# Top-k attention with a mixture of depths: slot search on GpSimd, the last products and the scatter one step sooner, and plain writes of the last rows

## The chip, the core and the metric

The kernel runs on one core of a Trainium2 chip. The core has a matrix engine (TensorE, PE in the profile, with its weight loads shown apart as PEld), a vector engine (VectorE, DVE), an activation engine (ScalarE, ACT), a general engine (GpSimd, POOL) and a queue for transfers (SyncE, SP). Each engine executes its own list of instructions in order and waits on semaphores for the others. The metric is the device time of one execution in microseconds; lower is better.

## The reference

There are 8 batches of 8 heads, 576 tokens and 64 features a head. Attention keeps, in each row, the 32 largest scores:

```python
scores = scale * np.matmul(q, k.transpose(0, 1, 3, 2))
kth = np.partition(scores, -top_k, axis=-1)[..., -top_k:-top_k + 1]
scores = np.where(scores >= kth, scores, -1e9)
attn = exp(scores - max) / sum            # then out = attn @ v
```

The heads' outputs of a batch, side by side, are `x` of 576 x 512. The second part, the mixture of depths, takes the 128 tokens of the batch with the largest gate score and adds to them a gated two-layer product:

```python
scores = x @ w_gate                        # one number a token
top_idx = 128 largest tokens of the batch
ye = np.maximum(x[top_idx] @ w1, 0.0) @ w2 # 512 -> 1024 -> 512
g = 1.0 / (1.0 + np.exp(-scores[top_idx]))
out[top_idx] = x[top_idx] + g[:, None] * ye
```

All other rows of `out` are `x`.

## The kernel before

**Units and steps.** A unit is a pair of heads with 128 rows of scores (or four half tiles for the last 64 rows). A batch has 18 units, the whole problem N = 144. The main loop goes over steps `n` from -1 to 143, and what follows writes i for `n % 18`. In step n every engine works on a different unit: TensorE multiplies the scores of unit n+1 (`multiply`), ScalarE copies them from PSUM to the tile `sc` (`keep`), VectorE searches unit n for a bound on the 32nd largest score (`find_bound`: 16 MAX8 on 72 columns each into `cand`, then MAX8 and MATCH_REPLACE8 on the candidates into `best`), ScalarE and GpSimd turn unit n-1 into `y`, the scores below that bound (`what_is_below`: `sides` is a sign with its count, `y` the product of scores and signs, `fill` 16 more columns), VectorE finds the exact 32nd largest of unit n-2 by two MAX8 on `y` (`find_kth`, result `next`), ScalarE and GpSimd each make half of the mask `less` of unit n-3 (`mask`), and TensorE transposes unit n-4 with the mask, ScalarE takes the exponential (`pT`, `last`) and TensorE multiplies it with the values into `av`.

**The order is written out by hand.** Engines are wrapped in `InOrder`, so the order of the code is the order on each engine. Three lists hold work to be put between: `vector_late` is flushed between the two halves of `find_bound`'s first loop (and after it), `late` goes to ScalarE ahead of `keep`, and `pool_late` goes to GpSimd after `find_bound` and ahead of `what_is_below`.

**Loads.** The rows of k and q of the next batch are transposed in half loads, one or two in a step, into the free columns of the score bank, and copied out by ScalarE (`kT`, `qT`). `loads_at[i]` says how many in step i, `first_loads` the same for the first batch; a batch has 18 of them.

**The mixture.** `mixture` is a generator of one batch, advanced at the end of those steps that `mix_at` lists (`mix_at_of` for the last two that run in the main loop), counted from the start of the following batch. Its stages are: `split` of the gates, and a row of all gates on every partition (`gate_row`); for each of 5 tiles of tokens `choose`, which counts how many gates are greater (`junk`, the rank in `ranks`) and then compares the rank with 0 to 127 (`pick`, the slot of each token); `multiply_places`, which turns picks into row numbers on TensorE; `fetch_rows`, a gather into `xe`; the transposes `xeT`; eight steps of `multiply_h`; eight of the product `y_ps`; then the scaled result `gy` on ScalarE and `add_rows`, an indirect DMA from GpSimd that adds 128 rows to `out` in memory. In a step with that scatter GpSimd is spared its half of the mask, which VectorE takes instead: the line `scatters = n % per_batch == 1 and n > 2 * per_batch`, so n = 37, 55, 73, 91, 109 and 127. `gates` is a dot product on VectorE (`prod` in the profile) for each tile of tokens that is done, after `normalise` (a reciprocal `rden`, then `x` on GpSimd).

**The tail.** After the loop the last four units are finished in an order of their own, and `closing` runs the mixture of the last batch, where each stage waits for the one before. Remaining stages of the batch before it, named `between`, are put in the gaps.

Of the kernel before, what the change touches and what calls it, by code (L numbers as in the profile page):

```python
# [10 lines left out]
AF = mybir.ActivationFunctionType  # L11
ALU = mybir.AluOpType
# [34 lines left out]
def kernel(  # L47
# [13 lines left out]
    B, H, S, D = q.shape  # L61
    HD = H * D
    F = moe_w1.shape[1]
    NHP = H // 2
# [7 lines left out]
    scale = 1.0 / float(D) ** 0.5 / SMALLER  # L72
# [92 lines left out]
    def load_weights():  # L165
# [6 lines left out]
    pe, dve, act, pool, sp = (  # L172
        InOrder(tc, e)
        for e in (nc.tensor, nc.vector, nc.scalar, nc.gpsimd, nc.sync)
    )


    late, vector_late, pool_late = [], [], []
# [410 lines left out]
    def mixture(row0, pg, rank, exact=False):  # L589
# [8 lines left out]
        if exact:  # L598
            for t0, t1, at in ((0, J, 0), (J, NT, JP)):
                tr = ps_misc.tile([P, 512], FP32, name="tr", tag="misc")  # L600
                n = R if t0 else P
# [6 lines left out]
                w = (t1 - t0) * n  # L608
                act.copy(out=gate_row[:, at : at + w], in_=tr[:, 0:w])
        else:  # L610
            row_dram = drampool.tile([1, S], FP32, name="row_dram")
            sp.dma_start(
                out=row_dram[0, 0:JP].rearrange("(p j) -> p j", j=J), in_=gate[:, 0:J]
            )
            sp.dma_start(
                out=row_dram[0, JP:S].rearrange("(p j) -> p j", j=1),
                in_=gate[0:R, J:NT],
# [5 lines left out]
        for t in range(NT):  # L623
            yield
            n = R if t == J else P

            def choose(t=t, n=n):
                junk = modpool.tile([P, S], FP32, name="junk", tag="scratch")
                dve.tensor_scalar(
                    out=junk[0:n, :],  # L630
                    in0=gate_row[0:n, :],
                    scalar1=gate[0:n, t : t + 1],
                    scalar2=None,
                    op0=ALU.is_gt,
                    op1=ALU.add,
                    accum_out=rank[0:n, t : t + 1],
                )
                if exact:
                    break_ties(t, gate, gate_row, rank)
                dve.tensor_scalar(  # L640
                    out=pick[0:n, t, :],
                    in0=slot[0:n, :],
                    scalar1=rank[0:n, t : t + 1],
                    scalar2=None,
                    op0=ALU.is_equal,
                )

            vector_late.append(choose)

        yield  # L650
        if exact:
            ps = ps_misc.tile([P, 512], FP32, name="place_ps", tag="misc")
        else:
            ps = values_bank[0]
        ps = ps[:, 2 * DE : 2 * DE + 6]
# [3 lines left out]
        row_i = modpool.tile([P, 1], I32, name="row_i", bufs=2)  # L659
        g = modpool.tile([P, 1], FP32, name="g", bufs=2)  # L660
# [27 lines left out]
        xe = modpool.tile([P, HD], FP32, name="xe")  # L688
# [4 lines left out]
        ps = ps_misc.tile([P, 512], FP32, name="xe_ps", tag="misc")  # L693
# [8 lines left out]
        for fc in range(NFC):  # L702
# [3 lines left out]
            if fc % 2 == 0:  # L706
                ps = ps_misc.tile([P, 2, CAP], FP32, name="h_ps", tag="misc")
# [8 lines left out]
        for fc in range(NFC):  # L716
            yield
            if fc == 0:
                ps = ps_misc.tile([P, 512], FP32, name="y_ps", tag="misc")
# [3 lines left out]
        gy = modpool.tile([P, HD], FP32, name="gy")  # L723
# [5 lines left out]
    def closing(b, pg, between):  # L729
# [51 lines left out]
        for t in range(J):  # L781
            dve.tensor_scalar(
                out=pick[:, t, :],
                in0=slot,
                scalar1=rank[:, t : t + 1],
                scalar2=others[:, t : t + 1],
                op0=ALU.subtract,
# [53 lines left out]
        for fc in range(NFC):  # L841
            pe.matmul(
                ps, hT[:, fc, :], w2[:, fc, :], start=(fc == 0), stop=(fc == NFC - 1)
            )
        gy = modpool.tile([P, HD], FP32, name="gy")
        w = HD // 2
        act.activation(gy[:, 0:w], ps[:, 0:w], AF.Copy, scale=g)
        dve.tensor_scalar_mul(gy[:, w:HD], ps[:, w:HD], g[:, 0:1])
        add_rows(gy, row_i)

    def multiply_places(ps, pick, pg):

# [45 lines left out]

    def add_rows(gy, row_i):

        pool.indirect_dma_start(
            out=out.flatten_outer_dims(),
            out_offset=bass.IndirectOffsetOnAxis(ap=row_i, axis=0),
            in_=gy,
            in_offset=None,
            compute_op=ALU.add,
        )

    def multiply_h(ps, fc, xeT):
# [38 lines left out]
    def store(ob, x):  # L948
# [11 lines left out]
    v_at = 6  # L960


    mix_at = (5, 7, 9, 10, 13, 14, 16, 16, *range(19, 34), 35, 36)


    mix_at_of = {
        B - 3: mix_at[0:8] + (19, 20, 20, 21, 21, 22, 22, 23, 24)
        + (25, 26, 26, 27, 27, 28, 28, 29),
        B - 2: (5, 7, 7, 8, 8, 8, 10, 10, 12, 13, 14, 15, 15, 16, 16, 17, 17),
    }  # L970

    loads_at = [1, 0, 0, *[1] * 11, 2, 2, 1, 1]
    first_loads = [0, 0, 1, *loads_at[3:]]
    assert sum(loads_at) == sum(first_loads) == 2 + 4 * NHP
    mix_steps = {}
    for b in range(B - 1):
        for i in mix_at_of.get(b, mix_at):
            mix_steps.setdefault((b + 1) * per_batch + i, []).append(b)

    place_steps = {}  # L980
    for b in range(B - 1):
# [51 lines left out]
    def mask_of(n, on=None):  # L1033
        b, i = divmod(n, per_batch)
        masks[n] = mask(scs[n], next8s[b][:, i, :, :], on)
        if i == per_batch - 1:
            at = 2 * per_batch * b
            pool.tensor_copy(
                out=seen[:, 1, at : at + 2 * per_batch].rearrange("p (n i) -> p n i", i=2),
                in_=next8s.pop(b)[:, :, :, 7],  # L1040
            )

    for n in range(-1, N):
        b, i = divmod(n, per_batch)
        if i == 0 and 0 <= b < B - 1:
            qkv[b + 1] = room_for_qkv(b + 1)
            loading = chain(
                loading, Rows(k[b + 1], q[b + 1], *qkv[b + 1][0:2]).parts()
            )
        if 0 < n + 1 < NHP:  # L1050
            turn_pair(first_rows, n + 1)
        if n == 1:
            load_v(v[0], qkv[0][2])
        if n == NHP:
            load_weights()


        gating = normalised
        if inverting is not None:
            normalised = inverting[0:2]  # L1060
            vector_late.insert(0, lambda a=inverting: normalise(*a))
            inverting = None
        else:
            normalised = None
        if gating is not None:
            vector_late.append(lambda a=gating: gates(*a))

        if is_unit(n - 4):  # L1070
            tr, av = room_to_turn()
            pT, last, exp = weigh(scs.pop(n - 4), tr, av, masks.pop(n - 4))
            exp()
        if is_unit(n - 3):

            scatters = n % per_batch == 1 and n > 2 * per_batch
            mask_of(n - 3, (act, dve) if scatters else None)
        flush()
        if is_unit(n + 1):
            b, t, g = units[n + 1]  # L1080
            ps = room_for_scores()
            multiply(t, g, *qkv[b][0:2], ps)
            b, i = divmod(n, per_batch)
            loads = list(islice(loading, first_loads[i] if b == 0 else loads_at[i]))
            halves = [ps[:, a, :, HALF : HALF + P] for a in range(2)]
            for load, half in zip(loads, halves):
                load[0](half)
            scs[n + 1] = keep(ps)
            for load, half in zip(loads, halves):
                load[1](half)  # L1090
        if is_unit(n - 4):
            b4, t4, g4 = units[n - 4]
            values(t4, g4, pT, last, av, qkv[b4][2])
            if n in place_steps:
                values_bank[0] = av
                next(mixtures[place_steps[n]])
            if g4 == 0:
                xs = xpool.tile([P, H, DE], FP32, name="xs")
                if t4 == 0:
                    x = xpool.tile([P, NT, HD], FP32, name="x")  # L1100
                    pg = gates_of[b4 % 2]
                    of_batch[b4] = x, pg
            keep_values(t4, g4, av, xs)
            if g4 == groups(t4) - 1:
                inverting = b4, t4, xs
                n4 = R if t4 == J else P
                keep_sums(n4, xs, sums[0:n4, b4 * NT + t4, :])
            while kept:
                kept.pop(0)()


        if is_unit(n):
            bests[n] = find_bound(scs[n])
        flush_vector()
        flush_pool()
        if is_unit(n - 2):
            kth_of(n - 2)
        while after_kth:
            after_kth.pop(0)()


        if is_unit(n - 1):
            what_is_below(n - 1)

        if gating is not None:
            b, t = gating
            if t == J:
                store(out[b], of_batch[b][0])
                mixtures[b] = mixture(float(b * S), of_batch[b][1], ranks[:, b, :])
        for b in mix_steps.get(n, ()):  # L1130
            next(mixtures[b], None)
        b, i = divmod(n, per_batch)
        if i == v_at and 0 <= b < B - 1:
            load_v(v[b + 1], qkv[b + 1][2])
# [55 lines left out]
    closed = closing(B - 1, pg, between)  # L1190
    next(closed)
    values_unit(N - 1)
    for _ in range(3):
        next(between)
    keep_unit(N - 1, xs)
    sums_of(J, xs)
# [156 lines left out]
```

## Time and profile before

| | before |
|---|---|
| time, median of 3 runs | 859.5 us (858.61 to 859.57) |
| span of the profile | 858.1 us |
| start of step 18, 36, 54, ... 126 on VectorE | 111.0, 210.4, 309.2, 408.0, 506.8, 605.6, 704.4 us |
| one batch in the steady part | 98.8 us |
| start of step 143, the last of the loop | 800.1 us |
| VectorE, ScalarE, GpSimd busy | 808.5, 761.0, 708.1 us |

In the profile's page, part 1 gives the busy time of each engine, part 5 the groups of equal instructions with their mean duration and the idle time ahead of them with what ended it. The stretches view gives the same busy times in windows of time, the waits view sums up who waited for whom, and the timeline lists instructions in order of start. On VectorE instructions overlap: the next starts before the last one's end is recorded. So what an instruction costs is the distance from its start to the start of the next, and not its duration.

### The profile page before, as it was taken

What the parts mean: (1) busy time and instruction counts of PE and PEld (TensorE: products, weight loads), DVE (VectorE), ACT (ScalarE), POOL (GpSimd) and SP (SyncE); (2) the same over time, 40 slices, a digit from 0 to 9 for tenths busy, and PEclk for the clock granted to TensorE, in tenths of its full rate; (3) what the DMA queues carried; (4) which work ended last, traced back from release to release, by engine and by line L of the source; (5) the groups of instructions that cost most, each with busy time, mean ns of one, the idle gap of its engine ahead of it and who ended that gap; (6) DMA issues with size and microseconds to landing.
All of it is one profiled execution on the core that took longest, in us unless ns stands there. A gap on an engine that the chain in (4) does not pass through costs nothing. (4 is left out here: it accounts for less than half of the span.)

```text
span 858.1 us, 28073 instructions
## 1 busy us (share of the span) xinstructions
PE 797.7 (93%) x9839; PEld 613.0 (71%) x9839; DVE 808.5 (94%) x4932; ACT 761.0 (89%) x1705; POOL 708.1 (83%) x699
## 2 busy tenths in 40 slices
PE   5799988988999999999999999999999999998976
PEld 4576666666787778877787777877788778767844
DVE  5899999999999999999999999999999999999850
ACT  3799999999999999999999999999999999978720
POOL 3599899888898899988898899988998888978720
PEclk9699999999999999999999999999999999999998
DMA  9921212421151221412233212512214102101021
GB/s 175 277 53 27 52 45 51 89 46 39 51 97 32 51 39 57 108 39 50 64 60 68 52 26 70 100 23 50 69 38 97 26 16 63 22 11 17 3 71 25
DMA packets 122196, 50.36 MB, mean 59 GB/s; under 512 B 116416, under 2 KB 116416, under 8 KB 121024
## 3 DMA queue, kind: packets, MB, share of 16 engines
q1 hardware_dynamic: 118672, 43.91, 21.9%
q0 software_dynamic: 1792, 4.20, 2.8%
q8 instruction: 79, 1.29, 0.6%
q14 instruction: 69, 0.57, 0.2%
q10 hardware_dynamic: 1584, 0.39, 0.2%
HBM read 36.93 MB, written 11.55 MB: 56 GB/s over the span
## 5 line engine op out<-in xcount | busy, mean ns | idle before, releaser
L43 POOL TENSOR_TENSOR y<-sc,sides 128x576 f32<-128x576 f32 x288 | 367.9, 1304 | 99.4 <-ACT sides L43 91.9
L43 DVE MAX8 cand<-sc 128x8 f32<-128x72 f32 x2304 | 330.2, 218 | 11.1 <-ACT sc L43 11.1
L43 POOL TENSOR_SCALAR less<-sc,next 128x576 bf16<-128x576 f32 x135 | 236.3, 1750 | 7.7 <-DVE next L43 5.0
L43 ACT ACTIVATE sides<-sc,seen 128x576 bf16<-128x576 f32 x288 | 221.0, 768 | 5.2
L43 PE MATMUL ptr<-out_of_reach,less 128*128 128x128 bf16 x1136 | 205.4, 220 | 19.6 <-POOL less L43 18.9
L43 PE MATMUL ptr<-ident,sc 128*128 128x128 f32 x1136 | 215.8, 280 | 0.0
L43 DVE MAX8 next<-y 128x8 f32<-128x584 f32 x288 | 204.5, 751 | 4.4 <-POOL y L43 4.3
L43 PE MATMUL ps<-kT,qT 64*128 64x288 f32 (+1 forms) x1280 | 184.6, 437 | 7.1 <-ACT qT L43 5.3
L43 PEld LDWEIGHTS av<-v,pT 128*64 128x64 f32 x4544 | 144.2, 137 | 46.1 <-ACT last L43 33.5
L43 PEld LDWEIGHTS ptr<-ident,sc 128*128 128x128 f32 x1136 | 160.8, 142 | 22.6 <-PE av L43 10.4
L43 PE MATMUL av<-v,pT 128*64 128x65 f32 x4544 | 163.9, 224 | 13.2 <-ACT last L43 11.8
L43 ACT COPY sc<-ps 128x1152 f32<-128x1152 f32 x144 | 160.6, 1115 | 11.8 <-PE ps L43 11.0
L43 PEld LDWEIGHTS <-less 128*128 128x128 bf16 x1296 | 133.3, 104 | 40.8 <-POOL less L43 26.0
L43 ACT ACTIVATE pT<-ptr 128x1024 f32<-128x1024 f32 x142 | 143.9, 1014 | 19.0 <-PE ptr L43 16.2
L43 DVE MAX8 best<-cand 128x8 f32<-128x24 f32 (+2 forms) x864 | 141.9, 200 | 0.0
L43 PEld LDWEIGHTS ps<-kT,qT 64*128 64x128 f32 (+1 forms) x1280 | 99.9, 180 | 46.8 <-issue 22.2
L43 ACT ACTIVATE less<-sc,next 128x576 bf16<-128x576 f32 x143 | 110.7, 774 | 12.6 <-DVE next L43 12.4
L43 DVE MATCH_REPLACE8 cand<-best,cand 128x24 f32<-128x24 f32 (+1 forms) x576 | 101.9, 185 | 0.0
L43 PE MATMUL av<-vpair,last 128*128 128x130 f32 (+1 forms) x314 | 68.1, 317 | 0.0
L43 PE MATMUL h_ps<-xeT,w 128*128 128x128 f32 x464 | 61.3, 277 | 0.3 <-ACT xeT L43 0.3
L43 PEld LDWEIGHTS h_ps<-xeT,w 128*128 128x128 f32 x464 | 55.8, 192 | 2.5 <-ACT xeT L43 1.4
L43 PE MATMUL y_ps<-w,hT 128*128 128x512 f32 x112 | 56.3, 596 | 0.0
(124 smaller groups left out, 848.2 us busy)
## 6 DMA issues: line engine op xcount, KB each, us to landing
v<-in_v_dram SPq DMA_DIRECT2D x64, 128.0 KB, 3.3
out_dram<-x SPq DMA_DIRECT2D x8, 1024.0 KB, 4.1
rows<-in_k_dram SPq DMA_DIRECT2D x56, 128.0 KB, 3.2
rows<-in_q_dram SPq DMA_DIRECT2D x56, 128.0 KB, 3.1
w<-in_moe_w_dram SPq DMA_DIRECT2D x2, 2048.0 KB, 13.5
gate_row<-row_dram SPq DMA_DIRECT2D x7, 288.0 KB, 4.5
w<-in_k_dram SPq DMA_DIRECT2D x8, 128.0 KB, 4.4
last<-in_k_dram SPq DMA_DIRECT2D x8, 128.0 KB, 3.6
```

Source lines behind the costliest of these rows:

```text
L43: return lambda *a, **kw: self._tc.keep_in_program_order(fn(*a, **kw))
```

## The change

There are four edits.

1. **Slots on GpSimd.** In `choose` the count stays on VectorE. The comparison that makes `pick` becomes `choose_slot`: tile 0 keeps it on VectorE, and the other four tiles of each batch put it into `pool_late`, so that GpSimd makes it after `find_bound` of the same step.
2. **One step sooner.** `mix_at` ends with steps 34 and 35 in place of 35 and 36, so the last two products, `gy` and the scatter come one step earlier (the scatter at i = 0, where it was at i = 1). `scatter_steps` now names the steps whose mask half VectorE takes: n = 54, 72, 90, 108, 126 and 137. Step 37, which had no scatter, is gone from it, and 137 is new. One half load moves from i = 16 to i = 1, with the stream of loads one behind.
3. **Last mixtures sooner.** `mix_at_of` begins most stages of the mixtures of batches 5 and 6 a step sooner. One stage of `between` moves from the gap before the last row's `keep_unit` to the loop in `closing` that finishes it.
4. **Last rows written.** In `closing` one VectorE instruction makes `gy = ps * g + xe`, in place of half a product on ScalarE and half on VectorE, and the rows are written over those in memory (`put_rows`) instead of being added there.

```diff
-                dve.tensor_scalar(
+                if t == 0:
+                    choose_slot(dve, t, n)
+                else:
+                    pool_late.append(lambda: choose_slot(pool, t, n))
+
+            def choose_slot(engine, t, n):
+                engine.tensor_scalar(
                     out=pick[0:n, t, :],
...
-        w = HD // 2
-        act.activation(gy[:, 0:w], ps[:, 0:w], AF.Copy, scale=g)
-        dve.tensor_scalar_mul(gy[:, w:HD], ps[:, w:HD], g[:, 0:1])
-        add_rows(gy, row_i)
+        dve.scalar_tensor_tensor(
+            out=gy, in0=ps, scalar=g[:, 0:1], in1=xe, op0=ALU.mult, op1=ALU.add
+        )
+        put_rows(gy, row_i)
...
-    mix_at = (5, 7, 9, 10, 13, 14, 16, 16, *range(19, 34), 35, 36)
+    mix_at = (5, 7, 9, 10, 13, 14, 16, 16, *range(19, 36))
...
-        B - 3: mix_at[0:8] + (19, 20, 20, 21, 21, 22, 22, 23, 24)
-        + (25, 26, 26, 27, 27, 28, 28, 29),
-        B - 2: (5, 7, 7, 8, 8, 8, 10, 10, 12, 13, 14, 15, 15, 16, 16, 17, 17),
+        B - 3: mix_at[0:8] + (18, 19, 20, 21, 21, 22, 23, 24, 24)
+        + (25, 25, 26, 26, 27, 27, 28, 28),
+        B - 2: (5, 6, 6, 7, 7, 7, 9, 9, 11, 12, 13, 14, 15, 16, 16, 17, 17),
...
-    loads_at = [1, 0, 0, *[1] * 11, 2, 2, 1, 1]
+    loads_at = [1, 1, 0, *[1] * 11, 2, 2, 0, 1]
...
+    scatter_steps = {
+        (b + 1) * per_batch + mix_at_of.get(b, mix_at)[-1] + 1 for b in range(B - 2)
+    }
...
-            scatters = n % per_batch == 1 and n > 2 * per_batch
-            mask_of(n - 3, (act, dve) if scatters else None)
+            mask_of(n - 3, (act, dve) if n in scatter_steps else None)
...
-    for _ in range(3):
+    for _ in range(2):
         next(between)
```

More of the change, by code (lines that the diff above doesn't have):

```diff
@@ L899, in add_rows, with put_rows @@
     def add_rows(gy, row_i):
+        put_rows(gy, row_i, compute_op=ALU.add)
+    def put_rows(rows, row_i, **how):
         pool.indirect_dma_start(
@@ L903, in add_rows @@
             out_offset=bass.IndirectOffsetOnAxis(ap=row_i, axis=0),
-            in_=gy,
+            in_=rows,
             in_offset=None,
-            compute_op=ALU.add,
+            **how,
         )
@@ L960 @@
     v_at = 6
-    mix_at = (5, 7, 9, 10, 13, 14, 16, 16, *range(19, 34), 35, 36)
+    mix_at = (5, 7, 9, 10, 13, 14, 16, 16, *range(19, 36))
     mix_at_of = {
-        B - 3: mix_at[0:8] + (19, 20, 20, 21, 21, 22, 22, 23, 24)
-        + (25, 26, 26, 27, 27, 28, 28, 29),
-        B - 2: (5, 7, 7, 8, 8, 8, 10, 10, 12, 13, 14, 15, 15, 16, 16, 17, 17),
+        B - 3: mix_at[0:8] + (18, 19, 20, 21, 21, 22, 23, 24, 24)
+        + (25, 25, 26, 26, 27, 27, 28, 28),
+        B - 2: (5, 6, 6, 7, 7, 7, 9, 9, 11, 12, 13, 14, 15, 16, 16, 17, 17),
     }
-    loads_at = [1, 0, 0, *[1] * 11, 2, 2, 1, 1]
+    loads_at = [1, 1, 0, *[1] * 11, 2, 2, 0, 1]
     first_loads = [0, 0, 1, *loads_at[3:]]
-    assert sum(loads_at) == sum(first_loads) == 2 + 4 * NHP
+    assert sum(loads_at) == sum(first_loads) + 1 == 2 + 4 * NHP
     mix_steps = {}
```

## The prediction

> **What bounds the kernel now.** I read the busy shares, then the stretches from batch to batch, then who waited for whom, and last the timeline of single steps.
>
> ```profile
> PE 797.7 (93%) x9839; PEld 613.0 (71%) x9839; DVE 808.5 (94%) x4932; ACT 761.0 (89%) x1705; POOL 708.1 (83%) x699
> ...
> 408.01:506.81 98.80, 97.24 (x1236) 75.38 (x1234) 98.44 (x614) 95.00 (x215) 87.84 (x85) 1.00 0.27 58
> ...
> 704.41:800.14 95.73, 91.41 (x1129) 71.41 (x1126) 95.34 (x581) 83.57 (x184) 82.48 (x80) 0.98 0.12 26
> 800.14:858.12 57.98, 43.09 (x400) 31.56 (x398) 25.48 (x97) 19.46 (x48) 18.62 (x22) 0.94 0.15 36
> ```
>
> The stretches are one steady batch, the last batch of the loop and the tail; after the length come PE, PEld, DVE, ACT and POOL. VectorE works 98.44 of 98.80 us, and in the last batch 95.34 of 95.73: it has no gap to fill. ScalarE has 3.8 us free in a batch, GpSimd 11. TensorE's 97.24 looks as full, but its matmuls are pipelined, so the waits decide:
>
> ```profile
> DVE cand L43 <- ACT sc L43: 2.3, 3, 1.4
> DVE next L43 <- POOL y L43: 1.6, 3, 0.8
> DVE prod L43 <- POOL x L43: 0.2, 1, 0.2
> ...
> ACT less L43 <- DVE next L43: 3.9, 12, 0.4
> ACT pT L43 <- PE ptr L43: 3.3, 15, 0.2
> ACT g L43 <- DVE g L43: 0.6, 4, 0.2
> ```
>
> The first three are all of VectorE's waits from 20 to 806 us, 4.1 us, the last three ScalarE's from 309 to 704 us (four batches). ScalarE waits for VectorE about 1.1 us a batch (3.9 + 0.6 over 4), VectorE hardly for anyone. From 107 to 806 us VectorE sets the pace.
>
> **What a pick costs.** The timeline of VectorE in a step that chooses:
>
> ```profile
> 461.38 1.16 DVE L43 MAX8 cand<-sc 128x8 f32<-128x72 f32 x8
> 462.45 0.80 DVE L43 TENSOR_SCALAR_CACHE_REDUCE junk<-gate_row,gate 128x576 f32<-128x576 f32 x1
> 463.17 0.08 DVE L43 DVE_READ_ACCUMULATOR junk<-gate_row,gate 128x1 f32 x1
> 463.29 0.29 DVE L43 TENSOR_SCALAR pick<-slot,ranks 128x128 bf16<-128x128 f32 x1
> 463.50 1.17 DVE L43 MAX8 cand<-sc 128x8 f32<-128x72 f32 x8
> ```
>
> From start to start, the count takes 0.72 us, its read-out 0.12 until the pick that needs it, and the pick 0.21. This step lasts 5.94 us (461.38 to 467.32), a plain one 4.90 (444.82 to 449.72). After a dot product the next MAX8 starts with the read-out (both at 781.32), so the 0.12 is the pick's wait. Without the pick a step saves 0.12 + 0.21 = 0.33 us.
>
> **What the Trainium skill says.** "SBUF — State Buffer", section "Who interferes with whom", states that VectorE and GpSimd share one pair of ports under an exclusive lock, which a VectorE instruction with two SBUF inputs contends for against GpSimd's reads. The trace agrees in part: the dot product `prod` has two such inputs and is the one whose duration swings, from 664 to 2760 ns, where MAX8 keeps its pace. The worst one, with GpSimd's line beside it:
>
> ```profile
> 778.62 2.76 DVE L43 CUSTOM_DVE_ANT_0 prod<-x,wg 128x512 f32<-128x512 f32 x1
> ...
> 776.30 1.63 POOL L43 DMA_INDIRECT out_dram<-gy,row_i  x1 [0.17 <-issue]
> 777.43 3.06 POOL L43 TENSOR_TENSOR y<-sc,sides 128x576 f32<-128x576 f32 x2
> ```
>
> "Perfetto Trace Analysis", section "Optimizing Scalar/DVE Operations", says that offloading from a saturated VectorE to GpSimd can make sense but, as they share a port, might not help. Here the work beside a moved pick is MAX8, which has one input, so I expect help. "DMA: Bandwidth & Descriptors", section "SDMA does more than copy", names a separate add unit for a DMA that adds; it gives no price for it.
>
> **The change, part by part.**
>
> Picks: four tiles in each of 7 mixtures leave VectorE, 28 x 0.33 = **-9.2 us**. On GpSimd one costs, by the line through `less` (576 columns, 1.75 us) and the 5-column cast (0.20), 0.20 + 128 x 0.0027 = 0.55 us, an estimate; 2.2 us a batch against 11 free. What is queued behind it is `y` of that step. At 463.29 the rank is known; GpSimd ends `less` at 464.32 and begins `y` at 465.50, waiting for ScalarE's `sides`. So the pick lies in that 1.17 us gap, in each of the four steps (gaps 1.2 to 1.5): hidden. In batch 6 three picks come in one step, 1.6 us, but VectorE there has `y` far ahead and three counts (2.2 us) of its own: hidden too. TensorE may wait for the last pick up to that 1.6 us; its lead covers it.
>
> Mask halves: VectorE's `less` takes 0.76 us to the next start in five of its six steps and 0.44 in the one at 709 us. Step 37 gives 0.76 back, step 137 takes 0.44 to 0.76. Net **-0.2**. The other five only move.
>
> The scatter at 776.30 follows `less` and `x` on GpSimd, so `y` is late and the dot at 778.62 loses 2.76 - 0.67 = 2.1 us. Now the scatter is a step away from `x`, and GpSimd is spared that `less`. Between 0 and -2.1, **-1.0**.
>
> Other dots: five a batch, which now fall at other points of GpSimd's work. In the steady batch they lose 0.55 us together (0.14 at i = 9, 0.41 at i = 13); in the first batch, where VectorE runs close behind ScalarE, 0.6 to 1.1 each. As VectorE speeds up it moves that way, but ScalarE, which waits for it, comes along. I take 0.25 a batch more, **+1.8**, between -2 and +8.
>
> ScalarE: its part in a batch can shrink by the 1.1 us it waits; VectorE's shrinks by 1.3. The moved half load and `gy` bring ScalarE's work out of i = 1 and 16 into 0, where it waited 0.37. VectorE's slack, `y` ready 2 to 4 us before it is read, takes the rest: I allow **+0.5**.
>
> Products and loads one step sooner: TensorE and ScalarE have the time at i = 16 and 0; nothing by itself.
>
> Tail: the end is one chain,
>
> ```profile
> 850.53 0.47 ACT L43 ACTIVATE gy<-ps,g 128x256 f32<-128x256 f32 x1 [6.54 <-PEq L1316]
> 851.04 0.48 DVE L43 TENSOR_SCALAR gy<-ps,g 128x256 f32<-128x256 f32 x1 [16.84 <-ACT gy L43]
> 851.80 1.56 POOL L43 DMA_INDIRECT out_dram<-gy,row_i  x1 [16.26 <-DVEq L1316]
> ```
>
> The two halves take 0.99 us. One instruction of 512 columns takes 0.48 + 256 columns at 1.04 ns (0.27), 0.75: **-0.2**; the 1.04 is the slope between MAX8 on 72 and on 584 columns, whose starts lie 0.134 and 0.667 us apart. The adding scatter lands 4.9 us after its start, the gather of equal size 3.5. A plain write lies between: 0 to -1.4, **-0.9**. The stage of `between` goes into the wait for the gather: nothing.
>
> Sum: -9.2 - 0.2 - 1.0 + 1.8 + 0.5 - 0.2 - 0.9 = -9.2, so 859.5 - 9.2 = **850.3 us**.
>
> **Rivals.**
> 1. ScalarE and TensorE become the bound. For it: in i = 5 to 13 `pT` waits for the transposes and ScalarE's steps are an even 5.44 us. Against it: the slack of 2 us. If only half of the 1.1 us is had in 6 batches (3.3), with 0.7 in the last batch and the tail's 1.1: -5.1, **854.4 us**.
> 2. The collisions go instead: no dot loses anything (7 x 0.5 = 3.5 in place of the +1.8), and the one in step 139 gains all of 2.1: about **844 to 847 us**.
> 3. Slower. Dots fall onto `y` as in the first batch: three a batch losing 0.9 more than now, 7 x 2.7 = 18.9 in place of 1.8, gives 850.3 + 17 = 867; two a batch, about **861 us**. Against it: the phase of GpSimd follows ScalarE, which follows VectorE.
> 4. GpSimd is late with `y` where a pick is queued ahead: it would show as VectorE waiting for `y`, 28 x 0.5 = 14 us at worst, **864 us**, against the 1.17 us gaps.
>
> **How the numbers follow.** Forecast 0.58, rival 1 0.22, rival 2 0.10, rivals 3 and 4 together 0.10, of which a third is partial and ends about even. The range from 846 to 856 takes in the forecast's unknowns (the write 1.4, the dot of step 139 2.1, dots 2 to 3) and rival 1. Faster by over 0.2% (below 857.8) 0.89, within it 0.04, slower 0.07.
>
> **What would show it.** Steady batches of about 97.5 us in place of 98.8, steps with a moved pick 0.33 shorter, VectorE still without gaps; `pick` on GpSimd near 0.55 us; the dot of step 139 under 2 us; the last scatter landing 3.5 to 4.9 us after its start. VectorE waits for `sc` or `y` from 200 to 700 us would say rival 1 or 4; longer `prod` would say rival 3.

## The result and the profile after

The changed kernel takes 853.1 us (median of 6 runs, 849.2 to 854.8), the kernel before 859.3 us beside it. The ratio is 0.9921, with a 95% interval from 0.9896 to 0.9947. A second measurement gave 853.8 us against 859.6, 0.9934 [0.9918, 0.9950]. So it is faster, by 0.5 to 1.0%. The forecast was 850.3, range 846 to 856.

The total came out near the forecast. Its parts did not. The page's busy shares, then the stretches view of the kernel after (the first, a middle and the last of the five steady batches, the last batch of the loop, the tail; length, then PE, PEld, DVE, ACT, POOL):

```profile
PE 791.2 (93%) x9839; PEld 610.5 (72%) x9839; DVE 806.8 (95%) x4904; ACT 761.2 (89%) x1704; POOL 727.5 (85%) x727
...
205.87:305.94 100.07, 97.57 (x1240) 75.75 (x1237) 99.06 (x610) 95.61 (x216) 91.74 (x90) 1.00 0.23 55
...
405.18:504.41 99.23, 97.18 (x1230) 75.43 (x1230) 99.01 (x610) 95.19 (x215) 91.05 (x89) 1.00 0.27 58
...
603.64:703.67 100.03, 97.26 (x1230) 75.42 (x1231) 99.57 (x610) 95.07 (x215) 91.08 (x89) 1.00 0.21 50
703.67:797.58 93.91, 90.72 (x1141) 72.22 (x1140) 92.32 (x578) 84.58 (x187) 84.65 (x84) 1.00 0.12 26
797.58:851.10 53.52, 40.72 (x374) 29.58 (x374) 24.27 (x97) 17.12 (x43) 15.55 (x20) 0.93 0.14 39
```

VectorE has four instructions less in the middle one (610 against 614), GpSimd four more (89 against 85). Yet the batch is longer: 99.23 us, where it was 98.80 and where 97.5 was forecast. VectorE is busy for 99.01 us of it, with less to do. The first and the last of the five are longer still, by 0.8 us each. The stretches of three profiles, from the starts of VectorE's `cand`, of the last gather and of the last write:

| stretch | before | after | after, second profile |
|---|---|---|---|
| to step 18 | 111.0 | 107.3 | 110.5 |
| steps 18 to 36 | 99.4 | 98.6 | 98.6 |
| steps 36 to 126, five batches | 494.0 | 497.8 | 497.5 |
| step 126 to 143 | 95.7 | 93.9 | 93.5 |
| 143 to the last gather | 29.6 | 26.8 | 26.8 |
| gather to the last write | 22.1 | 22.0 | 20.3 |
| write to the end | 6.3 | 4.8 | 4.8 |

The five steady batches lost 3.5 to 3.8 us, 2.2 to 2.5 us of it in the first and the last of them; the ends of the program won. Two rows are not the change's: up to step 16 the streams of instructions are the same, and between gather and write nothing was edited. There the granted clock differs, the figure after POOL's. These are the stretches from step 0 to 18 and from the gather to the write, of before, of after, and of after's second profile:

```profile
14.00:111.00 97.00, 82.70 (x964) 61.06 (x963) 91.02 (x580) 84.88 (x188) 73.51 (x67) 0.93 0.43 107
...
829.70:851.80 22.10, 17.90 (x89) 12.41 (x88) 4.39 (x21) 3.33 (x8) 2.69 (x2) 0.92 0.15 26
```

```profile
13.60:107.30 93.70, 78.60 (x963) 58.86 (x962) 91.09 (x581) 84.68 (x188) 73.58 (x67) 0.96 0.42 109
...
824.30:846.28 21.98, 18.79 (x91) 12.83 (x90) 4.66 (x21) 2.86 (x7) 2.70 (x3) 0.92 0.15 27
```

```profile
14.00:110.50 96.50, 81.95 (x959) 60.84 (x960) 90.41 (x576) 84.76 (x187) 73.56 (x67) 0.93 0.41 104
...
824.25:844.57 20.32, 17.46 (x97) 11.74 (x96) 6.21 (x30) 3.01 (x7) 2.70 (x2) 1.00 0.16 28
```

At clock 0.93 the start takes 97.0 and 96.5 us, at 0.96 it takes 93.7. The stretch behind the gather takes 22.0 us at 0.92 and 20.3 at 1.00, in one and the same kernel. In the fourteen profiles of this case it is 20.3 to 20.6 us at 1.00 and 21.8 to 22.2 at 0.92; the start goes the same way less strictly (from the first `cand` to step 18, 93.5 to 95.4 us at 0.96 and 95.4 to 97.7 at 0.93 to 0.95). So the 3.7 us that the first profile gains at the start are not counted for the change: the second has 0.5 of them.

Where a steady batch lost its time shows in the timeline at the step whose mask half VectorE makes, here in the kernel before (start, duration, engine), VectorE first:

```profile
411.57 1.42 DVE L43 MAX8 next<-y 128x8 f32<-128x584 f32 x2
413.10 0.84 DVE L43 TENSOR_SCALAR less<-sc,next 128x576 bf16<-128x576 f32 x1
413.85 0.76 DVE L43 MAX8 cand<-sc 128x8 f32<-128x72 f32 x5
...
411.10 2.52 POOL L43 TENSOR_TENSOR y<-sc,sides 128x576 f32<-128x576 f32 x2 [0.85 <-ACT sides L43]
```

And in the kernel after:

```profile
501.00 1.42 DVE L43 MAX8 next<-y 128x8 f32<-128x584 f32 x2
502.52 1.97 DVE L43 TENSOR_SCALAR less<-sc,next 128x576 bf16<-128x576 f32 x1
504.41 0.76 DVE L43 MAX8 cand<-sc 128x8 f32<-128x72 f32 x5
...
498.64 1.72 POOL L43 TENSOR_SCALAR less<-sc,next 128x576 bf16<-128x576 f32 x1
500.52 1.09 POOL L43 DMA_INDIRECT xe<-out_dram,row_i  x1 [0.16 <-DVE best L43]
501.63 2.53 POOL L43 TENSOR_TENSOR y<-sc,sides 128x576 f32<-128x576 f32 x2
```

The same instruction takes 0.75 us from its start to the next before and 1.89 after. In both it lets VectorE go on 0.23 to 0.25 us after GpSimd's pair of `y` has ended (413.62 and 504.16). This holds beyond one step. In the fourteen profiles 83 halves of `less` in this form on VectorE begin while an instruction of `y` runs, and all 83 let VectorE go on 0.21 to 0.42 us after the end of such an instruction, whether that took them 0.43 or 2.89 us; of 283 dot products that begin so, 275 do it 0.48 or 0.49 us after. So the five mask halves of the kernel before, at 0.76 us, were held already: in the one at 709 us, begun after both large instructions of `y`, it is 0.44. The waits view has nothing of all this:

```profile
DVE best L43 <- DVE cand L43: 0.2, 1, 0.2
```

That is all of VectorE's waits from 309 to 704 us, and ScalarE's largest there are these:

```profile
ACT pT L43 <- PE ptr L43: 5.5, 23, 0.3
ACT less L43 <- DVE next L43: 2.0, 4, 0.5
```

ScalarE waits less for VectorE than before (2.0 against 3.9) and more for TensorE's transposes (5.5 against 3.3). The dot products show the rest of a middle batch's loss, in the groups view from 309 to 704 us of before and of after (mean ns of one):

```profile
L43 DVE CUSTOM_DVE_ANT_0 prod<-x,wg 128x512 f32<-128x512 f32 x16 | 13.0, 811 | 0.0
```

```profile
L43 DVE CUSTOM_DVE_ANT_0 prod<-x,wg 128x512 f32<-128x512 f32 x16 | 14.9, 932 | 0.0
```

### The profile page after: what moved, and what is told of

Same layout as the page of the kernel before. It is cut to its first block, busy times and chain, and to the rows that moved or that the text cites. A ratio compares the mean times of both kernels' runs of the same rounds, so it can differ in the third digit from the quotient of the medians.

```text
span 851.1 us, 28068 instructions
## 1 busy us (share of the span) xinstructions
PE 791.2 (93%) x9839; PEld 610.5 (72%) x9839; DVE 806.8 (95%) x4904; ACT 761.2 (89%) x1704; POOL 727.5 (85%) x727
## 5 line engine op out<-in xcount | busy, mean ns | idle before, releaser
L43 POOL TENSOR_SCALAR less<-sc,next 128x576 bf16<-128x576 f32 x135 | 232.8, 1724 | 5.2 <-DVE next L43 4.5
L43 PE MATMUL ps<-kT,qT 64*128 64x288 f32 (+1 forms) x1280 | 181.0, 430 | 7.2 <-ACT qT L43 5.3
L43 PEld LDWEIGHTS ps<-kT,qT 64*128 64x128 f32 (+1 forms) x1280 | 98.1, 177 | 45.8 <-issue 21.9
```

Source lines behind the costliest of these rows:

```text
L43: return lambda *a, **kw: self._tc.keep_in_program_order(fn(*a, **kw))
```

## The experiments

Three things were to be told apart. Theory A: in the changed order the gather stands ahead of `y` on GpSimd, and edit 2 puts the mask half of VectorE beside that late `y`. Theory B, the port: a VectorE that is faster by the picks runs into GpSimd's `y` and is held there. Theory C, the pace: the other engines need some 98.4 to 99.2 us a batch, and what is taken from VectorE comes back as time in which it is held.

### Edit 1 alone, and all but edit 1

`picks_only` is the kernel before with edit 1. `no_picks` is the kernel after without it:

```diff
-                    pool_late.append(lambda: choose_slot(pool, t, n))
+                    choose_slot(dve, t, n)
```

> The kernel before with edit 1 alone (four of five slot searches on GpSimd, scatter still at i = 1). Theory A (the earlier scatter put VectorE's half of the mask behind a y that the gather delays): the picks keep their whole worth, steady batches 97.4 to 97.8 us in place of 98.8, VectorE's mask half stays near 0.76 us to the next start, total about 851 to 853. Rival B (a faster VectorE, or a pick ahead of y, is what makes the mask half fall on two y): the mask half goes to about 1.9 us, steady batches 98.6 or more, total 857 or more.

> The changed kernel with all slot searches back on VectorE; edits 2 to 4 stay. Theory A: VectorE's mask half stays at about 1.9 us and steady batches are 1.3 longer than the changed kernel's 99.23, so 100.3 to 100.6; total about 860 to 862. Rival B: the mask half is back at 0.76 and steady batches are about 99.4, total about 854.

Edit 1 alone gave 857.0 us, 0.9981 [0.9962, 0.9999]: 0.4 us a batch (98.45 against 98.80), with the mask half at 1.42 us and the dots' loss at 0.83 us. All but edit 1 gave 855.4 us, 0.9946 [0.9928, 0.9965], with 99.05 us a batch, the mask half at 0.44. Its timeline, VectorE and then GpSimd:

```profile
508.72 0.53 DVE L43 TENSOR_SCALAR less<-sc,next 128x576 bf16<-128x576 f32 x1
509.17 2.24 DVE L43 MAX8 cand<-sc 128x8 f32<-128x72 f32 x16
...
506.39 2.53 POOL L43 TENSOR_TENSOR y<-sc,sides 128x576 f32<-128x576 f32 x2
```

So in the steady batches the picks gain nothing in company (99.05 to 99.23). The first mixture, which has no scatter yet, keeps them whole: step 18 to 36 takes 99.40 before, 98.13 with edit 1, 99.79 without and 98.56 with all. In company the last batch of the loop gains as well: step 126 to 143 takes 96.4 us without edit 1 and 93.9 with all (alone it gains nothing there, 95.8 against 95.7). Theory A loses: with the gather and edit 2 as in the kernel after, the mask half is at its fastest once VectorE is slower and comes to it only 0.2 us before `y` ends.

### The gather behind `y`

```diff
-        flush_pool()
+        gather = n % per_batch == per_batch - 1
+        if not gather:
+            flush_pool()
...
+        if gather:
+            flush_pool()
```

> The changed kernel with the gather of i = 17 queued on GpSimd behind y of its step, where it stood ahead of it. Theory A: y of that step comes about 1.1 us sooner, VectorE's mask half takes 0.7 to 1.0 us in place of 1.88, steady batches 97.9 to 98.4 in place of 99.23, total 4 to 6 us less than the changed kernel. Rival B: the mask half stays at 1.9, steady batches 99.2, no difference.

870.1 us, 1.0126 [1.0100, 1.0152]. This run changed a second thing, which had not been thought of: the scatter of the next step now follows directly on the gather in GpSimd's queue. Its waits from 309 to 704 us, and what TensorE waits for there:

```profile
POOL out_dram L43 <- DVE cand L43: 7.6, 2, 3.9
POOL out_dram L43 <- DVE next L43: 3.7, 1, 3.7
POOL out_dram L43 <- ACT last L43: 3.4, 1, 3.4
```

```profile
PE ptr L43 <- POOL less L43: 14.2, 4, 3.8
```

GpSimd stands still for 3.4 to 3.9 us once a batch ahead of the scatter. The releasers named were done long before, and the stop is about as long as a gather needs to land (3.5 us by the page). The same pair stands in the kernel after: behind its last gather, at 824.3 us, a scatter follows directly, and there the profile names the gather's DMA for a stop of 3.2 us. So the landing is the likely cause; a run with another instruction between wasn't made. VectorE, too, waits for the late `y` here, 10.8 us in the four batches. On theory A the run says only that the mask half fell to 0.96 us: it goes on after the first instruction of `y`, not after both. So the place of the gather counts for the size of the hold, but it isn't what brought it.

### The mask half without VectorE

```diff
-            mask_of(n - 3, (act, dve) if n in scatter_steps else None)
+            mask_of(n - 3, None)
```

> The changed kernel with GpSimd making its half of the mask in the scatter's step too, so that VectorE never makes one in the loop. Theory A: VectorE is rid of 1.88 us a batch, GpSimd has 1.7 us more in front of scatter and y; with y 2 us ahead VectorE does not wait, steady batches 97.4 to 98.2. Rival (GpSimd needs to be spared there): y comes late, VectorE waits for y or a dot at i = 3 meets two y, steady batches 99 or more.

852.5 us, 0.9936 [0.9905, 0.9967]. In the middle three batches the 1.88 us are gone from VectorE and the batch is shorter by 0.1 us (99.15). The dots' loss rose from 1.14 to 2.08 us, and the one pick that VectorE still makes, which takes 0.21 us from its start to the next, took 1.23. What was taken off came back elsewhere within the batch. The first and the last of the five did gain, 2.1 and 0.9 us, and the last batch of the loop lost it again (96.5 us in place of 93.9). Besides, TensorE waits 1.6 us a batch for that mask half of GpSimd.

### The mask half in another form

The same comparison, in the form that also sums its results:

```diff
+            elif engine is dve and lone:
+                below = stats.tile([P, 1], FP32, name="below")
+                dve.tensor_scalar(
...
+                    op0=ALU.is_lt,
+                    op1=ALU.add,
+                    accum_out=below,
+                )
```

> The changed kernel, but VectorE's half of the mask in the loop is the form that also sums its output (an unused sum)[...]. Lock theory (the 1.88 us are the shared port, held by GpSimd's two y): it takes about 0.8 us with its read-out, steady batches 98.2 to 98.8 in place of 99.23, total 3 to 6 us less than the changed kernel. Semaphore theory (it waits for a tile or for GpSimd's order): it stays near 1.9 us and batches at 99.2. Pace theory (ScalarE and TensorE set the pace and only hold VectorE by way of the lock): the 1.1 us come back in the dots or as waits, batches 99.0 or more.

850.1 us, 0.9897 [0.9863, 0.9930]; 98.61 us a batch. The timeline, VectorE and then GpSimd:

```profile
503.88 0.81 DVE L43 TENSOR_SCALAR_CACHE_REDUCE less<-sc,next 128x576 bf16<-128x576 f32 x1
504.62 0.08 DVE L43 DVE_READ_ACCUMULATOR less<-sc,next 128x1 f32 x1
504.62 1.04 DVE L43 MAX8 cand<-sc 128x8 f32<-128x72 f32 x7
...
502.96 2.53 POOL L43 TENSOR_TENSOR y<-sc,sides 128x576 f32<-128x576 f32 x2
```

`y` stands beside it as in the kernel after, begun 0.9 us earlier. Now VectorE goes on after 0.74 us, 0.87 us before the end of `y`. The same comparison beside the same neighbour isn't held in this form, so the semaphore theory falls and the form decides, as a lock on the shared ports would have it. Of the 1.14 us won, 0.5 went back into the dots (1.14 to 1.63).

### The products and the scatter at their old steps

Edit 2 is undone for batches 0 to 3:

```diff
-    mix_at = (5, 7, 9, 10, 13, 14, 16, 16, *range(19, 36))
+    mix_at = (5, 7, 9, 10, 13, 14, 16, 16, *range(19, 34), 35, 36)
+        B - 4: mix_at[0:8] + tuple(range(19, 36)),
...
-    loads_at = [1, 1, 0, *[1] * 11, 2, 2, 0, 1]
+    loads_at = [1, 0, 0, *[1] * 11, 2, 2, 1, 1]
```

> The changed kernel with edit 2 undone for batches 0 to 3: last products at 35 and 36, scatter and mask half at i = 1, half loads as before. If the earlier step by itself costs time: batches 2 to 4 as in the run with the picks alone, 98.3 to 98.5 in place of 99.23, total 2 to 4 us less than the changed kernel. If the earlier step is what gains: batches 99.5 or more.

851.1 us, 0.9904 [0.9873, 0.9934]. The batches from step 18 on take 98.20, 97.85, 97.56, 98.47, 98.78 and 100.53 us. The third is the shortest, with the mask half at 0.76 and 0.58 us in the dots; then the holds are back (1.43 and 0.82 at 98.78). The first five are 0.4 to 2.2 us shorter than those of the kernel after; the last, where the schedules meet again and two mask halves fall, is 0.5 longer. The run moves the products, the mask half and the half load together, so which of them costs is open.

### Edit 4 undone, edit 3 undone

`add_end` puts the two half products and `add_rows` back into `closing`. `old_last_mixtures` puts the lists of `mix_at_of` and the three stages of `between` back.

> The changed kernel with edit 4 undone: two halves of gy and an adding scatter at the end. From the trace of the changed kernel the end of the span is then 1.5 us later after the scatter's start (6.3 in place of 4.8) and the start itself 0.2 later: total 1.5 to 1.9 us more than the changed kernel, batches the same. If the write is no quicker than the adding one: 0.2 us.

> The changed kernel with edit 3 undone. If edit 3 is what shortened the way from step 143 to the last gather (26.8 us in place of 29.6): that way is back at 29 to 30 us and step 139's dot at 2 us or more, total 3 to 5 us more. If the picks did it: 27 us, no difference.

With edit 4 undone: 854.5 us, 0.9954 [0.9938, 0.9971]. The batches are unchanged (99.25). Timelines of the end, `add_end` first, then the kernel after:

```profile
844.38 0.47 ACT L43 ACTIVATE gy<-ps,g 128x256 f32<-128x256 f32 x1 [6.54 <-PEq L1330]
844.88 0.48 DVE L43 TENSOR_SCALAR gy<-ps,g 128x256 f32<-128x256 f32 x1 [15.25 <-ACT gy L43]
845.65 1.56 POOL L43 DMA_INDIRECT out_dram<-gy,row_i  x1 [14.66 <-DVEq L1330]
```

```profile
845.25 0.75 DVE L43 SCALAR_TENSOR_TENSOR gy<-ps,g,xe 128x512 f32<-128x512 f32 x1 [16.39 <-PEq L1330]
846.28 1.00 POOL L43 DMA_INDIRECT out_dram<-gy,row_i  x1 [16.07 <-DVEq L1330]
```

From the start of `gy` to that of the write it is 1.27 against 1.03 us, from there to the end 7.0 (6.3 in the kernel before) against 4.8. With edit 3 undone: 855.5 us, 0.9957 [0.9936, 0.9979]; step 143 to the gather takes 28.0 us instead of 26.8 (with edit 1 alone, too, it is 28.0, and 29.6 before), the dot of step 139 1.48 instead of 0.94.

### Combinations, beside the kernel after

`late_accum` joins the old steps and the other form of the mask half. `accum_dots` has that form, and each dot product at the end of `find_bound`'s first loop, no longer in its middle:

```diff
+        while dots:
+            dots.pop(0)()
...
-            vector_late.append(lambda a=gating: gates(*a))
+            dots.append(lambda a=gating: gates(*a))
```

`late_accum_dots` has all three.

> The changed kernel once more, beside the next three on one chip. Both theories: 852 to 855 us, steady batches of 99.2 us, VectorE's mask half 1.9 us from its start to the next.

> The mask half in its accumulating form and the products, scatter and loads of batches 0 to 3 at their old steps. Port theory (what VectorE loses, it loses to GpSimd's y and to nothing else): nothing holds the mask half, it takes 0.7 to 0.8 us in every batch, and the batches take 97.6 to 98.2 us, as the raw work of VectorE would have it. Pace theory (ScalarE and TensorE need about 98.4 us, and VectorE is held until it agrees with them): after two or three batches the slack is used up, the dot products or waits for sc take what the mask half gave, and the last of batches 3 to 6 stand at 98.4 to 98.8. The time by the first theory 845 to 848, by the second 849 to 852 us.

> The accumulating mask half and, besides, the dot product of each tile moved from the middle of the first loop of find_bound to its end, so that it meets another part of GpSimd's step. Port theory: the dots that fall clear of y lose at most 0.5 us per batch together, in place of 1.6, the batches take 97.2 to 97.8 us. Pace theory: the batches stay at 98.2 to 98.7, and where the dots lose nothing, waits of VectorE for sc or y appear in their place (over 0.3 us per batch).

> All three: accumulating mask half, old steps for products, scatter and loads of batches 0 to 3, dot products behind the first loop. Port theory: 97.0 to 97.8 us per batch and 844 to 847 us, faster than any version so far. Pace theory: not below 98.2 us per batch once the slack of the first batches is used up, 848 to 851 us, VectorE with waits for sc or y.

| | time | ratio to before | a steady batch |
|---|---|---|---|
| the kernel after | 853.8 | 0.9934 [0.9918, 0.9950] | 99.23 |
| late_accum | 849.8 | 0.9889 [0.9852, 0.9925] | 98.46 |
| accum_dots | 850.9 | 0.9916 [0.9884, 0.9948] | 98.61 |
| late_accum_dots | 846.1 | 0.9857 [0.9825, 0.9888] | 98.03 |

The dots of `accum_dots` lose 0.72 us a batch in place of 1.63, and the batch is what it was without that edit, 98.61. The other 0.9 us are in one instruction, VectorE's own `pick`, which now falls beside `y` (VectorE, then GpSimd):

```profile
448.47 1.22 DVE L43 TENSOR_SCALAR pick<-slot,ranks 128x128 bf16<-128x128 f32 x1
449.61 1.17 DVE L43 MAX8 cand<-sc 128x8 f32<-128x72 f32 x8
...
447.08 2.52 POOL L43 TENSOR_TENSOR y<-sc,sides 128x576 f32<-128x576 f32 x2 [1.12 <-ACT sides L43]
```

It takes 1.14 us in place of 0.21. The pace theory had the time right and the form wrong: no wait for `sc` or `y` appeared, the hold moved from one instruction to another. With the old steps as well, 98.03 us a batch is below the 98.2 that theory gave as a floor, and above the 97.8 of the other; the next batch, where the schedules meet and two mask halves fall, takes 98.9. `late_accum_dots` is the fastest version here; its interval lies below the changed kernel's.

## Why the prediction was right or wrong

One subtraction orders most of it. From a steady batch take what VectorE spends in the three kinds of instructions that `y` can hold: the mask half, the dots above 0.60 us, and VectorE's own picks above 0.21 (start to next start). What remains is the same within 0.2 us in every version of one kind, those with all picks on VectorE and those with one:

| batch from step 90 | batch | mask half | dots | picks | rest |
|---|---|---|---|---|---|
| before | 98.80 | 0.76 | 0.56 | -0.04 | 97.52 |
| no_picks | 99.05 | 0.44 | 1.13 | -0.01 | 97.49 |
| picks_only | 98.45 | 1.42 | 0.83 | 0.02 | 96.19 |
| after | 99.23 | 1.88 | 1.15 | 0.02 | 96.19 |
| pool_mask | 99.18 | 0 | 2.09 | 1.02 | 96.07 |
| mask_accum | 98.60 | 0.74 | 1.62 | 0.01 | 96.23 |
| accum_dots | 98.61 | 0.74 | 0.73 | 0.92 | 96.23 |
| late_accum_dots | 98.03 | 0.74 | 1.04 | 0.04 | 96.22 |

Two things lie outside it. In `gather_behind` VectorE also waits for `y`, 2.7 us a batch. And in the kernel after the batches from steps 36 and 108 come to a rest of 97.1 and 96.5 us: single small instructions of VectorE take up to 0.5 us longer there, and the cause of that is open.

- **Picks, -9.2.** The price was right: the rest falls by 1.3 us a batch, 0.33 for each of four. `pick` on GpSimd takes 0.61 us (0.55 estimated) and no wait for `y` follows from it; here its instructions in the kernel after, with the shortest, median and longest in ns:

```profile
L43 POOL TENSOR_SCALAR pick<-slot,ranks x28: 599/611/622, 163.8 to 751.9; 128x128 bf16<-128x128 f32 x21, 64x128 bf16<-64x128 f32 x7
```

  But of the 1.3 us saved in a steady batch, edit 1 alone kept 0.35 and in company nothing. The ends kept it: 1.2 us in the first mixture and, in company, 2.5 in the last batch of the loop.
- **Mask halves, "the other five only move".** This is the step that failed. The mask half went from 0.76 to 1.88 us in the steady batches. I had taken what it cost before for its own price, while it was held then too (0.44 free), and watched only two-input instructions for the lock. That the dot is "the one whose duration swings" was a misreading: the mask half (0.44 and 0.76) and the picks (0.20 to 0.35 on 128 rows) swung in the same trace. "SBUF — State Buffer", section "Who interferes with whom", says that `tensor_scalar`, though not the form that writes out its accumulator, can enter modes that use the shared pair where its operands allow it, and that the loser is then blocked, not slowed. The runs agree: 1.89 us and 0.74 us beside the same `y`, and 0.21 to 1.14 for the pick. Which mode the comparison was in, no run shows.
- **Other dots, +0.25 a batch.** The direction was right, the size was 0.59.
- **Products and loads one step sooner, "nothing by itself".** Wrong. Undoing it shortens five of six batches by 0.4 to 2.2 us, and `late_scatter` took 2 to 2.7 us less than the kernel after did in either of its measurements, though the intervals overlap.
- **The dot of step 139, -1.0.** 2.69 to 0.94 us, -1.75. That edit 3 is behind a part of it shows in the 1.48 without it.
- **The tail.** `gy` -0.2 came as worked out (1.27 to 1.03). The write gave -1.5 beside the kernel before and -2.2 beside `add_end`, for -0.9, past its bound of -1.4. The sooner mixtures, counted at nothing, are worth 1.2 us between step 143 and the gather.
- **ScalarE, +0.5, and VectorE without gaps.** VectorE shows no gaps, and that was read as a sign of the bound. It is not: a VectorE that is held is recorded as busy.
- **The rivals.** The third's mechanism (VectorE falls onto `y`) came true, in the mask half more than in the dots: 1.12 + 0.59 = 1.7 us a steady batch, where it reckoned with 1.8 to 2.7. It ended on the other side because it counted this for all seven mixtures, while the ends of the program won. The first named ScalarE and TensorE, and was close in time (854.4). The second was near for the dot of step 139 and wrong for the others. The fourth did not come: VectorE has no wait for `y` from 309 to 704 us. What sets the 98 to 99 us isn't settled. That VectorE alone doesn't is shown by `accum_dots` and `pool_mask`, where in the middle batches what was taken off it came back as holds within 0.1 us. Which of ScalarE, TensorE and GpSimd does was not tried by itself.

In sum: the five steady batches were to give between 5 and 6.5 us and took 3.5 to 3.8. The first mixture gave 0.8, the last batch with the stretch to the last gather 4.6 to 5.0, the write 1.5. That is 3.2 to 3.8 us of the 5.9 to 6.2 by which the medians differ.

The rest goes with the granted clock, whose mean is on record for most executions. Within one kernel the time falls as it rises: the kernel before took 859.7 us at a mean of 0.986 (median of 28) and 856.4 at 0.992 (12). All 26 executions of the kernel after lie at 0.989 or more, of the kernel before only 26 of 69. Among those between 0.989 and 0.992 the medians are 857.6 us (21) and 854.2 (18). They are 3.3 us apart, as the stretches say, where the forecast had 9.2. Whether the change itself raises the clock, or the executions fell so, isn't shown.

So the total fell into the forecast's range by luck. Its mechanism, that a VectorE with less to do makes each steady batch shorter, failed; the ends of the program and the clock made up for it.

## What to carry to other kernels

On an engine that shows no gaps, ask what an instruction takes beside each neighbour, not what it takes on average: before moving work off VectorE, look which of its instructions come to lie beside GpSimd's, and compare their distance from start to start. If a batch doesn't get shorter by what was removed, subtract the instructions that can be held and see whether the rest fell. Compare two kernels by executions of the same mean clock where it is on record: here this took 6 us down to 3.3. A changed form of the instruction can be worth more than its place: adding an unused sum to one comparison was worth 0.6 us a batch.

## What the runs showed of the hardware

- A comparison from f32 to bf16 on VectorE, 576 columns, one input, took 0.44 us when both large instructions of GpSimd's `y` were over. Begun during one of them, it lets VectorE go on 0.21 to 0.42 us after the end of that instruction or of the next one of the pair (83 of 83 cases, up to 2.89 us); in the form with a sum it takes 0.74 us beside the same `y`. A dot product goes on 0.48 or 0.49 us after (275 of 283 cases).
- The hold runs both ways: GpSimd's `y` of 16 columns took 0.66 us beside a dot product, 0.44 beside the plain comparison and 0.22 otherwise.
- The last indirect write of 128 rows took 1.00 us on GpSimd, the one that adds 1.56. From its start to the end of the program it was 4.3 to 5.1 us in the eleven profiles that write and 6.3 to 7.0 in the three that add.
- The same stretch of the tail takes 20.3 to 20.6 or 21.8 to 22.2 us with the granted clock, and the start 93.5 to 97.7: a single profile's stretch can't be taken for the change's.
